# Kernel for a gated mix of a state-space convolution and a spectral filter: the order of work in its last part

## The chip, the cores and the metric

The kernel runs on one core of a Trainium2 chip. The metric is the device time of one execution in microseconds (us). The kernel before was timed three times: 625.73, 626.65 and 628.19 us; the median is 626.65. The execution that was profiled took 633.86 us, of which 631.9 us lie between its first and its last instruction (the span).

## What is computed

The input u has 2048 positions and 640 channels. Two branches work on it, and a gate per position mixes them. This is the reference, cut to what matters:

```
def _A_ref(u, log_A_real, A_imag, C_real, C_imag, log_dt, D_skip):
    dt = jnp.exp(log_dt)
    A = -jnp.exp(log_A_real) + 1j * A_imag
    C = (C_real + 1j * C_imag) * dt[:, None]
    P = jnp.exp((A * dt[:, None])[:, :, None] * pos[None, None, :])
    K = 2.0 * jnp.einsum("dn,dnl->dl", C, P).real
    Kf = jnp.fft.rfft(K, 2 * L)
    Uf = jnp.fft.rfft(u_t, 2 * L)
    y = jnp.fft.irfft(Uf * Kf[None], 2 * L)[:, :, :L]
    return y.transpose(0, 2, 1) + u * D_skip

def _B_ref(x, w_r, w_i):
    X = jnp.fft.rfft2(x, axes=(-2, -1)) * (w_r + 1j * w_i)
    return jnp.fft.irfft2(X, s=(S, D), axes=(-2, -1))

g = sigmoid((u * gate_w).sum(-1, keepdims=True))
return g * _A_ref(u, ...) + (1 - g) * _B_ref(u, w_r, w_i)
```

## The kernel before

All Fourier transforms are written as matmuls with tables of sines and cosines, in two stages each (32 blocks by 64 positions). The channels are worked in four parts of 160; the index c below names the part. Much is handed from stage to stage through DRAM.

The first two thirds of the span belong to parts that the change hardly touches: the forward transform of u, stored as the tensor u_d; the whole spectral branch up to its last inverse stage, stored as s3e_d; and the convolution kernel K, stored as k_d. `phase_c` then starts the transform of K for c = 0. `phase_d` is the last part of the program, from about 440 us on, and it is this part that the change rewrites.

`phase_d` has 16 units (c, u): four parts of the channels, and four groups of frequencies u within each. A unit goes through these steps.

- **Load**: `load` brings the spectra of u for this unit into the tile us (three buffers), on ScalarE's DMA queue (L813, L815).
- **First stage of K** (`T.first`, which runs `stage1`, L365 and L366): ten groups of matmuls for each c, spread over the four units of c - 1. ScalarE copies each group from PSUM into the tile t1. The tile kt that feeds it is loaded by `load_k` on SyncE's queue.
- **Front** (`fronts`): `spectra` makes a group of frequencies with four matmuls (L378; the one group 16 has two, L822). VectorE multiplies it by us twice (L835, L836), and for every two groups VectorE subtracts (L838) and GpSimd adds (L839); the product is the tile t2.
- **Back** (`backs`): the first inverse stage, 32 matmuls into a PSUM tile pi of four banks with one buffer (L855), two copies by ScalarE into s3 (L858, two buffers), and a store to the tensor s3_d on ScalarE's queue (L859).

Two kinds of last stages run beside the units. `last_e` takes the tile t3e, which `load_e` loads from s3e_d (L890), in six groups of two matmuls for each c (`halved`, L190), and VectorE writes each group times 1 - g to oe (L912). `last_c` takes the tile t3, which `load_c` loads from s3_d in four pieces (L902), in six groups for each c (L929); the result times g plus oe is the output (L934, L935, L932), which is stored.

PSUM has one pool, ps, of four banks for everything but the back; spectra, first stages and last stages take its banks in turn.

What sets the order: each unit's streams (fronts and backs; last stages; first stages) are generators, and `merge` draws from them by given times, which fixes only the order of the program's text. The tile framework then schedules: it orders each engine's instructions by its own estimates, so that an engine's order differs from the text. `behind(T.mm)` asks that a last stage be issued after the latest back's matmul. Backs follow their fronts by two units (`late`), from unit 13 on by one. Queues are in order: an instruction that waits holds all that stand behind it on its engine, and the same goes for DMA issues on SyncE's queue (SP) and on ScalarE's.

After the last unit comes the close: remaining backs, loads of the last pieces of t3, `last_c` for c = 2 and then for c = 3, and their stores.

Of the kernel before, what the change touches and what calls it, by code (L numbers as in the profile page):

```python
# [15 lines left out]
SYNC = mybir.DependencyInfo(mybir.DependencyClass.Sync, mybir.DependencyReason.DATA)  # L16
DRAM = bass.MemoryType.DRAM
# [165 lines left out]
class Ctx:  # L183
    pass

# [580 lines left out]
def phase_c(tc, A, T, ctx):  # L766

    nc = tc.nc
    V, G, S = nc.vector, nc.gpsimd, nc.scalar
# [6 lines left out]
    T.t1, T.kt, T.ki = {}, {}, {}  # L776
    T.w3 = T.cc.tile([128, 17, 2, 64], F32, name="w3")

    def load_k(c, h):
        if c < 4:  # L780
            T.kt[c, h] = T.kp.tile([128, 20, 64], F32, tag="k", name="kt")
            T.ki[c, h] = nc.sync.dma_start(T.kt[c, h][:, :, :], T.k_d[c, :, 20 * h:20 * h + 20])

    def first(c, ps):
        t1 = T.t1[c] = T.tp[c % 2].tile([128, 16, 160, 2], F32, tag="t1", name="t1")
        t1v = t1.rearrange("p x d y -> p d x y")
        for h in range(2):
            yield from stage1(nc, ps, T.e1, lambda q: T.kt[c, h][:, q, :], 20, t1v[:, 80 * h:80 * h + 80], S.copy)
            load_k(c + 1, h)

    T.load_k, T.first = load_k, first
    load_k(0, 0)
    load_k(0, 1)
    with tc.tile_pool(name="c_ps0", side="right", reuse_waits="tile", bufs=3, space=PSUM) as ps:
        yield from first(0, ps)


def phase_d(tc, A, T, ctx, out):
    nc = tc.nc
    V, G, S, P = nc.vector, nc.gpsimd, nc.scalar, nc.tensor  # L800
# [9 lines left out]

    def load(c, u, st):
        us = st.us = up.tile([128, 5, 2, 160], F32, tag="us", name="us")
        nc.scalar.dma_start(us[:, 0:4], T.u_d[c, :, 4 * u:4 * u + 4])  # L813
        if u == 2:
            nc.scalar.dma_start(us[32:64, 4], T.u_d[c, 32:64, 16])  # L815
# [9 lines left out]
    def fronts(c, u, st):  # L825
        t2 = st.t2 = wk.tile([128, 5, 2, 160], F32, tag="t2", name="t2")
        gs = GROUPS[u]
        for h in range(0, len(gs), 2):
            hn = min(2, len(gs) - h)
            l = slice(0, 128) if hn > 1 else slice(32, 64)  # L830
            ma = wk.tile([128, 2, 2, 160], F32, tag="ma", name="ma")
            mb = wk.tile([128, 2, 2, 160], F32, tag="mb", name="mb")
            for i in range(hn):
                pv = spectra(c, gs[h + i])[l]
                V.tensor_tensor(out=ma[l, i], in0=pv, in1=st.us[l, h + i], op=ALU.mult)  # L835
                V.tensor_tensor(out=mb[l, i], in0=pv, in1=st.us[l, h + i, ::-1, :], op=ALU.mult)  # L836
                yield 0.55
            V.tensor_tensor(out=t2[l, h:h + hn, 0], in0=ma[l, :hn, 0], in1=ma[l, :hn, 1], op=ALU.subtract)  # L838
            G.tensor_tensor(out=t2[l, h:h + hn, 1], in0=mb[l, :hn, 0], in1=mb[l, :hn, 1], op=ALU.add)  # L839

    def backs(c, u, st):
        t2, gs = st.t2, GROUPS[u]
        s3 = w2k.tile([128, 4, 320], F32, tag="s3", name="s3")
        p = pi.tile([128, 4, 512], F32, tag="pi", name="p_i2")
        for j in range(2):
# [7 lines left out]
            for ri in range(2):  # L853
                for o, l, i in todo:
                    T.mm = P.matmul(o, T.w3[l, gs[i], ri], t2[l, i, ri], start=ri == 0, stop=ri == 1)  # L855
            yield 0.55
        for s in (0, 2):
            S.copy(s3[:, s:s + 2], p[:, s:s + 2, 0:320])  # L858
        T.sd = nc.scalar.dma_start(T.s3_d[c, 32 * u:32 * u + 32].rearrange("(x k) a d -> (k a) x d", k=4), s3.rearrange("p s (j d) -> p (s j) d", j=2))  # L859
        yield 0.1  # L860

    groups = [(c, u) for c in range(4) for u in range(4)]
    late, sts, t3s, t3es, oes = [], {}, {}, {}, {}

    def mains(i):

        for y in groups[i + 1 if i else 0:i + 2]:
            sts[y] = Ctx()
            load(*y, sts[y])
        x = groups[i]  # L870
        yield from fronts(*x, sts[x])
        late.append(x)
# [140 lines left out]
```

## Time and profile before

| what | value |
|---|---|
| time, median of three | 626.65 us (625.73 to 628.19) |
| the profiled execution's own time | 633.86 us |
| its span | 631.9 us |
| mean granted TensorE clock | 0.926 |
| TensorE (PE) busy | 540.1 us (85%) |
| VectorE (DVE) busy | 463.1 us (73%) |
| ScalarE (ACT) busy | 362.9 us (57%) |
| GpSimd (POOL) busy | 235.8 us (37%) |
| HBM, read and written | 157 GB/s over the span |

The shares are means over the span. A page of the profile also shows the span in 40 slices of 15.8 us; the last twelve of these are `phase_d`, and in them the engines are busy by turns. What bounds that part is read from its stretches and from the chain of work that ended last: each step of this chain is followed back to what released it. In a row of the chain stand the start, the length and the piece of work, with its tile and line. In a table of stretches stand, for each engine, the busy us and in brackets the number of instructions, then the granted TensorE clock (1.00 is full speed), the mean busy share of the 16 DMA engines and GB/s. "PEld" is TensorE's loading of weights.

### The profile page before, as it was taken

The numbers are of one execution on the slowest core, as the hardware profiler recorded it, in microseconds if no ns is written. First come the engines' busy times: TensorE is split into PE (matmuls) and PEld (weight loads), VectorE is DVE, ScalarE is ACT, GpSimd is POOL, SyncE is SP. The second block draws the span as 40 slices with busy tenths as digits, with TensorE's granted clock in tenths as the row PEclk, the third lists the DMA queues.
The fourth block names the chain that finished last, engine by engine and source line by source line (L and its number), as shares of the span: only waits on it lengthen the run. The fifth ranks groups of instructions, "written<-read, shape, count | busy, mean of one in ns | idle before, by whom it ended". The sixth has DMA issues, their size and how long they took to land.

```text
span 631.9 us, 17674 instructions
## 1 busy us (share of the span) xinstructions
PE 540.1 (85%) x7580; PEld 396.9 (63%) x7580; DVE 463.1 (73%) x780; ACT 362.9 (57%) x655; POOL 235.8 (37%) x214
## 2 busy tenths in 40 slices
PE   9687979988989989987989988999499659849974
PEld 7675647765757666766776855668377446636641
DVE  6960597597899999999989899783376328408853
ACT  4644675486857689796878887977123211311220
POOL 4921153053436436344255253152122126107341
PEclk9888998999979999999879999979799959959987
DMA  8776203236612413232502320046848846764896
GB/s 341 304 272 211 65 27 123 90 128 194 229 43 63 135 44 113 84 135 65 154 2 72 92 107 23 26 137 214 319 146 311 286 139 219 289 204 146 271 303 244
DMA packets 47334, 100.66 MB, mean 159 GB/s; under 512 B 3204, under 2 KB 32280, under 8 KB 45368
## 3 DMA queue, kind: packets, MB, share of 16 engines
q1 hardware_dynamic: 24600, 66.69, 30.6%
q10 hardware_dynamic: 19616, 22.19, 10.9%
q0 software_dynamic: 3040, 10.65, 5.0%
q8 instruction: 60, 0.98, 0.6%
q14 instruction: 18, 0.15, 0.1%
HBM read 59.70 MB, written 39.81 MB: 157 GB/s over the span
## 4 chain that ended last, share of the span: by engine, by line
PE 53%; DVE 20%; DMA 14%; issue 5%; ACT 5%; POOL 2%; DVEq 0%; SPq 0%; ACTq 0%; POOLq 0%
PE p_s L365 9%; PE p_s L378 9%; PE p_eo L581 7%; PE p_e L668 5%; DMA t3e<-s3e_d 4%; PE p_k L725 4%; DMA s_d<-s 4%; DMA u_d<-ut 4%; DVE q L682 3%; PE p_e L190 3%; PE p_i L855 3%; PE p_t L532 3%; PE p_p L679 2%; PE p_c L929 2%; PE p_i L595 2%
## 5 line engine op out<-in xcount | busy, mean ns | idle before, releaser
L378 PE MATMUL p_s<-t,w 128*64 128x160 f32 x1040 | 97.3, 324 | 10.6 <-ACT ut L412 7.5
L378 PEld LDWEIGHTS p_s<-t,w 128*64 128x64 f32 x1040 | 77.1, 144 | 24.3 <-ACT ut L412 8.4
L710 POOL TENSOR_TENSOR y<-e,sc 128x512 f32<-128x512 f32 x40 | 55.5, 1386 | 93.9 <-DVE x L705 52.5
L670 ACT ACTIVATE e<-p_e 128x512 f32<-128x512 f32 x120 | 68.6, 601 | 23.6 <-PE p_e L668 21.4
L366 ACT COPY t<-p_s 128x512 f32<-128x512 f32 x40 | 24.4, 618 | 89.7 <-PE p_s L365 89.7
L725 PE MATMUL p_k<-x,y 128*32 128x64 f32 x2560 | 63.4, 227 | 11.1 <-POOL y L710 6.1
L581 PE MATMUL p_eo<-td,pmt 107*128 107x321 f32 x204 | 68.7, 457 | 3.0 <-ACT pmt L535 3.0
L712 POOL TENSOR_TENSOR y<-e,sc 128x512 f32<-128x512 f32 x40 | 55.4, 1386 | 41.2 <-ACT sc L696 31.2
L725 PEld LDWEIGHTS p_k<-x,y 128*32 128x32 f32 x2560 | 45.4, 112 | 40.0 <-issue 24.0
L839 POOL TENSOR_TENSOR t<-mb 128x320 f32<-128x320 f32 (+1 forms) x36 | 34.6, 962 | 79.0 <-DVE mb L836 65.1
L682 DVE SCALAR_TENSOR_TENSOR q<-q,p_p 128x512 f32<-128x512 f32 x80 | 53.1, 678 | 12.8 <-ACT q L681 12.5
L668 PE MATMUL p_e<-rm,par 128*128 128x512 f32 x120 | 59.6, 525 | 3.2 <-ACT e L670 3.0
L835 DVE TENSOR_TENSOR ma<-p_s,us 128x320 f32<-128x320 f32 (+1 forms) x68 | 33.1, 487 | 35.8 <-PE p_s L378 35.6
L681 ACT ACTIVATE q<-p_p 128x512 f32<-128x512 f32 x80 | 46.6, 592 | 6.0 <-PE p_p L679 5.6
L581 PEld LDWEIGHTS p_eo<-td,pmt 107*128 107x128 f32 x204 | 38.7, 199 | 17.9 <-ACT pmt L535 5.2
L707 DVE TENSOR_TENSOR x<-e,cx 128x1024 f32<-128x1024 f32 x40 | 48.4, 1210 | 1.6 <-ACT cx L698 1.6
L365 PEld LDWEIGHTS p_s<-c,kt 128*64 128x64 f32 x640 | 39.5, 144 | 14.0 <-issue 11.2
L679 PE MATMUL p_p<-rp,par 128*128 128x512 f32 x80 | 43.5, 549 | 5.0 <-DVE q L682 4.9
L929 PE MATMUL p_c<-t,c 128*64 128x480 f32 (+1 forms) x96 | 23.9, 615 | 25.9 <-issue 20.1
L858 ACT COPY s<-p_i 128x640 f32<-128x640 f32 x32 | 20.6, 695 | 44.1 <-DMA s_d<-s 18.5
L365 PE MATMUL p_s<-c,u 128*64 128x128 f32 x640 | 43.1, 285 | 2.5 <-ACT ut L412 2.5
L365 PE MATMUL p_s<-c,kt 128*64 128x128 f32 x640 | 43.9, 285 | 0.9 <-ACT q L681 0.7
(152 smaller groups left out, 1105.6 us busy)
## 6 DMA issues: line engine op xcount, KB each, us to landing
u_d<-ut SPq DMA_DIRECT2D x32, 320.0 KB, 3.2
us<-u_d ACTq DMA_DIRECT2D x16, 640.0 KB, 6.0
s_d<-s ACTq DMA_DIRECT2D x16, 640.0 KB, 5.7
t<-s_d SPq DMA_DIRECT2D x14, 640.0 KB, 6.3
ww<-in_w_l SPq DMA_DIRECT2D x8, 642.0 KB, 4.0
ue<-u_d SPq DMA_DIRECT2D x8, 640.0 KB, 4.3
k_d<-kt SPq DMA_DIRECT2D x4, 1280.0 KB, 8.7
kt<-k_d SPq DMA_DIRECT2D x8, 640.0 KB, 5.3
```

What stands on the lines that cost most here:

```text
L365: nc.tensor.matmul(p[64 * ri:64 * ri + 64, j, :], src(i + j), e1[ri], start=True, stop=True)
L378: ins = nc.tensor.matmul(p[64 * j:64 * j + 64, i, 160 * ri:160 * ri + 160], w2[:, x, 64 * ri:64 * ri + 64], t1[:, x // 2 if x < 32 else K0 ...
L581: P.matmul(p[:, :E], st.pmt[:DC, c, w, j, :], tv[:DC, w, c, :], start=c == 0, stop=c == 2)
L668: P.matmul(p[:, :], pars[t], rm[:, c:c + 512], start=True, stop=True)
L670: st.exp = S.activation(ef[:, c:c + 512], p[:, :], AF.Exp)
L679: P.matmul(p[:, :], pars[t], rp[:, c:c + 512], start=True, stop=True)
L681: S.activation(qf[:, c:c + 512], p[:, :], AF.Copy, bias=MAGIC)
L682: V.scalar_tensor_tensor(out=qf[:, c:c + 512], in0=qf[:, c:c + 512], scalar=MAGIC, in1=p[:, :], op0=ALU.subtract, op1=ALU.subtract)
L707: V.tensor_tensor(out=x[:, 0].rearrange("p d (h j) -> p d h j", h=2), in0=e[:, :, 0:64].rearrange("p d (h j) -> p d h j", h=2), in1=cx.uns ...
L710: ins = G.tensor_tensor(out=y[:, 1], in0=e[:, :, 64:96], in1=sc[:, 0], op=ALU.mult)
L712: G.tensor_tensor(out=y[:, 0], in0=e[:, :, 64:96], in1=sc[:, 1], op=ALU.mult)
L725: P.matmul(st.pb[32 * r:32 * r + 32, o, :], y[:, ri, 4 * qq + JR[r], :], x[:, ri, 4 * qq + JR[r], :], start=t % 2 + qq + 1 - ri == 0, stop ...
```

## The change

`phase_d` is written as one loop over the 16 units, and every engine keeps the order of that text. For this, the class `Pinned` wraps an engine: each instruction gets an order-only dependence (NOSYNC, which makes no wait on a semaphore) on the one issued before it through the same wrapper. Instructions made in `phase_d` therefore carry line L197, the line of the wrapper, in the changed kernel.

In the loop, the back of unit n - 1 (`inverse`) stands in the middle of unit n. Last stages move to later units: `last_e` stands in the third and fourth unit of c = 0, and in the second and third of each further c; `last_c(c - 1)` has its first half in the fourth unit of c and its second half in the first unit of c + 1. The loads of us are issued two units ahead (the first three by SyncE, in `phase_c`), and the table w3 is loaded in `phase_c` too, ahead of them. In the close, all loads of t3 are issued by SyncE.

```
+class Pinned:
+    def __init__(self, tc, eng):
+        self.tc, self.eng, self.last = tc, eng, None
+    def __getattr__(self, name):
+        f = getattr(self.eng, name)
+        def call(*args, **kw):
+            ins = f(*args, **kw)
+            if self.last is not None:
+                self.tc.add_manual_dep(ins.ins, self.last.ins.name, NOSYNC, reason="order")
+            self.last = ins
+            return ins
+        return call
...
 def phase_c(tc, A, T, ctx):
...
+    def load_u(eng, c, u):
+        if c < 4:
+            us = T.us[c, u] = T.up.tile([128, 5, 2, 160], F32, tag="us", name="us")
+            eng.dma_start(us[:, 0:4], T.u_d[c, :, 4 * u:4 * u + 4])
+            if u == 2:
+                eng.dma_start(us[32:64, 4], T.u_d[c, 32:64, 16])
...
     load_k(0, 1)
+    nc.sync.dma_start(T.w3[:, :, :, :], A["t_w3s"].rearrange("p (g r m) -> p g r m", g=17, r=2))
+    for u in range(3):
+        load_u(nc.sync, 0, u)
...
 def phase_d(tc, A, T, ctx, out):
...
+    nc = PinnedCore(tc)
...
+    def pair(c, u, h):
...
+        pvs = [spectra(c, g)[l] for g in gs]
+        for i in range(n):
+            V.tensor_tensor(out=ma[l, i], in0=pvs[i], in1=us[l, h + i], op=ALU.mult)
+            V.tensor_tensor(out=mb[l, i], in0=pvs[i], in1=us[l, h + i, ::-1, :], op=ALU.mult)
+        V.tensor_tensor(out=t2[l, h:h + n, 0], in0=ma[l, :n, 0], in1=ma[l, :n, 1], op=ALU.subtract)
+        G.tensor_tensor(out=t2[l, h:h + n, 1], in0=mb[l, :n, 0], in1=mb[l, :n, 1], op=ALU.add)
...
-        while len(late) > (1 if i > 12 else 2):
-            yield from backs(*late[0], sts.pop(late.pop(0)))
...
-            if g - (c == 0) in (0, 1):
-                beside = [last_e(c, AG * (g - (c == 0)))]
-            if c and g == 1:
-                load_c(c - 1, 0, 64)
-            if c and g == 2:
-                load_c(c - 1, 64, 64)
-            if c in (1, 2) and g > 1:
-                beside += [last_c(c - 1, AG * (g - 2))]
...
+    for n, (c, g) in enumerate(units):
+        if g == 0:
+            fst = T.first(nc, c + 1, ps) if c < 3 else iter(())
+        if g == 1 and c:
+            for u in range(3):
+                load_c(c - 1, u)
+        if g == 2 and c:
+            load_c(c - 1, 3)
+        if n == 15:
+            load_c(3, 0)
+        beside = []
+        if g - (c == 0) in (1, 2):
+            beside = last_e(c, AG * (g - 1 - (c == 0)))
+        elif g == 3 and c < 3:
+            beside = last_c(c - 1, 0)
+        elif g == 0 and c > 1:
+            beside = last_c(c - 2, AG)
+        beside = iter(beside)
+        pair(c, g, 0)
+        next(fst, 0)
+        if n and n < 14:
+            T.load_u(S, *units[n + 2])
+        next(beside, 0)
+        pair(c, g, 2)
+        next(fst, 0)
+        if n:
+            inverse(*units[n - 1])
+        next(beside, 0)
+        if len(GROUPS[g]) > 4:
+            pair(c, g, 4)
+        if g != 2:
+            next(fst, 0)
+        next(beside, 0)
+        for _ in beside:
+            pass
+        if g - (c == 0) == 2:
+            load_e(c + 1)
+    inverse(3, 3)
+    load_c(3, 1)
+    load_c(3, 2)
+    load_c(3, 3, 2)
...
```

Three places show what the change does to the engines' orders. The first is TensorE's order at the first last stage of the spectral branch (p_e from the tile t3e). Before, in the second unit:

```order
L365 MATMUL p_s_5650<-c_65,kt 64x128 x8
L378 MATMUL p_s_5666<-t_5276,w_68 64x160 x4
L855 MATMUL p_i_5827<-t_5592,w_5268 64x160 x32
L190 MATMUL p_e<-t3e,c_65 64x480 x2
L365 MATMUL p_s_5678<-c_65,kt 64x128 x8
```

Now, in the second unit and at the start of the third (p_s from t is a group of spectra, p_s from kt a group of the first stage, p_i the back):

```order
L197 MATMUL p_i_5723<-t_5595,w_5268 64x160 x32
L197 MATMUL p_s_5761<-c_65,kt 64x128 x8
L197 MATMUL p_s_5774<-t_5284,w_68 64x160 x4
L197 MATMUL p_s_5779<-t_5284,w_68 64x160 x4
L197 MATMUL p_s_5790<-c_65,kt 64x128 x8
L197 MATMUL p_e<-t3e,c_65 64x480 x2
```

The p_e group stood right behind the back of the first unit; now the rest of the second unit and half of the third lie between the two. From the first group of spectra to this p_e there were five groups of spectra, three of the first stage and a back; now there are ten, seven and a back.

The second place is TensorE's order at the first last stage of the convolution branch (p_c from the tile t3, here t_6083 or t_6110). Before, with c = 1, behind the first group of spectra of its third unit:

```order
L378 MATMUL p_s_6215<-t_5602,w_68 64x160 x4
L855 MATMUL p_i_6296<-t_5965,w_5268 64x160 x32
L855 MATMUL p_i_6405<-t_6089,w_5268 64x160 x32
L929 MATMUL p_c<-t_6083,c_65 64x480 x2
L365 MATMUL p_s_6228<-c_65,kt 64x128 x8
L378 MATMUL p_s_6238<-t_5602,w_68 64x160 x4
```

Now, in the fourth unit of c = 1:

```order
L197 MATMUL p_s_6359<-t_5614,w_68 64x160 x4
L197 MATMUL p_s_6364<-t_5614,w_68 64x160 x4
L197 MATMUL p_s_6375<-c_65,kt 64x128 x8
L197 MATMUL p_c<-t_6110,c_65 64x480 x2
L197 MATMUL p_s_6395<-t_5614,w_68 64x160 x4
L197 MATMUL p_s_6400<-t_5614,w_68 64x160 x4
```

Before, two backs in a row and then p_c stood ahead of the rest of the third unit, which stands behind p_c in the queue; now p_c stands one unit later, and no two backs stand together until the close.

The third place is SyncE's queue, which issues these loads. Before (k_d is the last store of K, t3 the piece that p_c needs):

```order
L735 DMA k_d_60<-kt_4654 128x2560
L890 DMA t3e_5585<-s3e_d_58 128x2560
L902 DMA t3_6083<-s3_d_59 32x5120
L782 DMA kt_5733<-k_d_60 128x1280
L890 DMA t3e_5863<-s3e_d_58 128x2560
L782 DMA kt_5942<-k_d_60 128x1280
L902 DMA t3_6083<-s3_d_59 32x5120 x2
```

Now:

```order
L761 DMA k_d_60<-kt_4654 128x2560
L197 DMA t3e_5593<-s3e_d_58 128x2560
L197 DMA kt_5759<-k_d_60 128x1280
L197 DMA kt_5994<-k_d_60 128x1280
L197 DMA t3e_6000<-s3e_d_58 128x2560
L197 DMA t3_6110<-s3_d_59 32x5120 x3
```

The first piece of t3 no longer stands ahead of the loads of kt and of the second t3e; three pieces of t3 follow each other behind them.

More of the change, by code (lines that the diff above doesn't have):

```diff
@@ L979, in phase_d @@
-    for y in late:
-        run(backs(*y, sts[y]))
-    with behind(T.sd):
-        load_c(3, 64, 32, eng=nc.scalar)
-    load_c(3, 96, 32, 2)
-    run(last_c(2, 0))
-    run(last_c(2, AG))
+    units = [(c, u) for c in range(4) for u in range(4)]
+    load_e(0)
+    for n, (c, g) in enumerate(units):
[35 more added lines that the diff above has]
+            load_e(c + 1)
```

154 lines of the change are left out of this document (55 added, 99 removed).

## The prediction

> **What bounds the kernel now.** I read the slices of the page first, then the chain of waits, then the stretches that the chain points to.
>
> ```profile
> span 631.9 us, 17674 instructions
> PEclk9888998999979999999879999979799959959987
> ```
>
> The granted clock drops to 5 in two of the last twelve slices. The chain says why; it starts for my purpose at the last part's first spectra (the timeline's row, 440.05).
>
> ```profile
> 440.05 0.79 PE L378 MATMUL p_s<-t,w 128*64 128x160 f32 x8 [0.51 <-ACT t L366]
> ```
>
> ```profile
> 441.06 13.91 DMA t3e<-s3e_d
> ...
> 494.79 11.49 DMA t3e<-s3e_d
> 506.28 6.60 issue
> 512.89 1.87 PE p_c L929 x4
> 514.76 1.71 PE p_s L365 x16
> 516.47 2.13 PE p_s L378 x16
> ...
> 549.87 9.42 DMA s_d<-s
> 559.29 4.81 issue
> ...
> 598.22 7.93 DMA s_d<-s
> ...
> 607.56 2.52 PE p_i L855 x64
> ```
>
> Between the waits the chain runs on TensorE alone. It stops four times: at the first t3e, twice ahead of a p_c whose t3 is not there, and at a store of s3. "issue" behind the transfers is the rest of the same waits: the piece of t3 can only be loaded once the store has landed. SyncE's own waits say it too:
>
> ```profile
> SPq L902 <- DMA s_d<-s: 105.0, 12, 15.3
> ```
>
> Next, the stretches (PE, PEld, DVE, ACT, POOL busy, clock, DMA share, GB/s):
>
> ```profile
> 441.00:632.00 191.00, 145.16 (x2214) 102.51 (x2210) 100.95 (x231) 39.17 (x62) 55.80 (x57) 0.86 0.71 241
> 441.00:455.00 14.00, 6.03 (x142) 5.50 (x138) 5.01 (x12) 3.18 (x5) 2.05 (x2) 0.83 0.99 388
> 495.00:513.00 18.00, 4.75 (x180) 3.49 (x176) 1.01 (x3) 4.46 (x7) 0.24 (x1) 0.77 0.92 309
> 550.00:564.00 14.00, 3.70 (x128) 2.90 (x128) 0.10 (x1) 2.57 (x4) 0.00 (x0) 0.59 0.88 282
> 523.00:543.00 20.00, 19.75 (x271) 14.29 (x269) 14.37 (x33) 5.01 (x8) 9.89 (x11) 1.00 0.81 277
> 465.00:495.00 30.00, 30.00 (x476) 22.50 (x474) 22.85 (x52) 8.15 (x14) 8.44 (x9) 1.00 0.70 237
> 611.40:632.00 20.60, 9.71 (x44) 3.44 (x40) 9.66 (x23) 0.00 (x0) 5.74 (x5) 0.81 0.74 264
> ```
>
> TensorE is idle for 8.0, 13.3 and 10.3 us in the three stalls, while DMA works hard; where TensorE flows, DMA has a rest (0.70, 0.81). So the last part is bound by turns: TensorE where it flows, transfers where it stops.
>
> **The change, part by part.** With the fixed order, p_e and p_c stand a unit and more behind the moves that feed them. I rebuild the last part from TensorE's rows at full clock:
>
> ```profile
> 520.86 0.69 PE p_s L822 x4
> ...
> 530.52 0.81 PE p_e L190 x4
> 531.32 0.87 PE p_s L365 x16
> 532.20 1.14 PE p_s L378 x16
> ...
> 545.42 0.73 PE p_i L855 x32
> 546.15 0.69 PE p_e L190 x4
> ...
> 548.53 0.02 issue
> ```
>
> A pair of spectra costs 1.14, a first-stage group 0.87, a last-stage group of 480 columns 0.81 and one of 320 columns 0.69, a back 2 x 0.73 = 1.46, group 16 0.69. From unit 0 to the last back the new order holds 32 pairs (36.5 us), 30 first-stage groups (26.1), 24 last-stage groups of 480 (19.4) and 12 of 320 (8.3), 16 backs (23.4) and four of group 16 (2.8): 116.5 us. `last_c` of c = 2 and 3 lies in the close, as before.
>
> How much longer than such a sum does a flowing stretch take? From 512.89 to 548.53 the old order ran 8 groups of 480 and 4 of 320, 9 first-stage groups, 15 spectra, the matmuls of two backs and one group 16: 6.5 + 2.8 + 7.8 + 8.6 + 2.9 + 0.7 = 29.3 us. It took 35.6, of which the first three rows, at the low clock, are 1.87 + 1.71 + 2.13 - (0.81 + 0.87 + 1.14) = 2.9 too long. That leaves 32.7, a factor of 1.12. Part of that excess is backs cut into single matmuls between other groups, which the new order keeps whole; I take 1.10, with 1.00 and 1.12 as ends. So 116.5 becomes 128 us (116.5 to 130.5), and unit 0's start at 440.05 plus 128 is 568.
>
> For the rest of the sum I need ScalarE's copies of the back and the landing times of loads:
>
> ```profile
> t3e<-s3e_d SPq DMA_DIRECT2D x4, 1280.0 KB, 7.2
> us<-u_d ACTq DMA_DIRECT2D x15, 640.0 KB, 6.2
> w<-in_t_w3s SPq DMA_DIRECT2D x1, 1088.0 KB, 10.0
> L858 ACT COPY s<-p_i 128x640 f32<-128x640 f32 x32 | 20.6, 695 | 44.1 <-DMA s_d<-s 18.5 <-PE p_i L855 16.7 <-DVE oe L912 7.2
> ```
>
> Behind the last unit comes the close. The last back waits for ScalarE's two copies of the one ahead, 2 x 0.70 by the row above, about 1.5 with its signals. From the end of the last back (607.56 + 2.52 = 610.08) to the end of the span there were 21.8 us: copies, store, load, two matmul groups, the last multiply-adds, the store of the output. The change leaves this chain alone, and the stall at 598.22 goes: the s3 buffer then waited for was held by a store two backs old, and now backs are a unit apart.
>
> What the new order moves into the way: **t3e for c = 1** is issued behind the last p_e of unit 3, and needed in unit 5. Between stand three pairs, four first-stage groups and a back, 3.4 + 3.5 + 1.5 = 8.4 us, or 9.2 with the factor. Such a load took 11.5 us in the chain above (7.2 in the middle, by the same rows). The cost is between 0 and 2.3 us; I take 1.5, nearer to the 11.5, since three pieces of t3 and a kt go with it. The first t3e lands at 455 as before or up to 6 us sooner, since w3 and two tiles us (2.4 MB, at 388 GB/s) now go ahead of 441; it is needed after 5.7 + 6.1 + 1.5 = 13.3 us of rows, 14.6 with the factor, at 454.7: nothing. The other loads have a unit or two: a unit is 8 us, a load 6.
>
> VectorE, ScalarE and GpSimd do the same work as before. In the flowing 30 us from 465 they were busy for 22.9, 8.2 and 8.4 us beside TensorE's 30.0, so they hide; if VectorE lost that cover, it could become the bound only where it has over a third more to do.
>
> The sum: 440.05 + 128 + 1.5 + 1.5 + 21.8 = 593 for the span, 39 less than 631.9, and 595 for the profiled execution's own time of 633.86. That execution was 7.2 us above the median of the runs, so I carry the 39 over: 626.65 - 39 = **588**. Its own range runs from a factor of 1.00 and no new wait (575) to 1.12 with the wait (591), and a little beyond for what no row shows.
>
> One rule speaks against this. The Trainium skill, "TensorE: Matmul & The Clock Gate", section "A second HAM failure mode: psum-queue depth-cycling", says that a kernel that cycles through PSUM banks can leave TensorE idle so often for moments that its clock swings between half and full. The new order cycles through four banks all along. This trace speaks against the rule here: from 465 to 495 the same four banks were cycled and the clock was 1.00. By the row the sum is as above; by the rule it would grow as in the last rival below.
>
> **The rivals.**
>
> *Transfers become the bound.* From 441 on DMA was busy 0.71 x 191 = 136 us. About 7 of them (2.4 MB at 277 / 0.81 = 342 GB/s) move ahead of 441, and 0.74 x 20.6 = 15 lie in the close, which leaves 113 to be done in 128 us, a share of 0.88. For it: the best 20 us in which TensorE flowed had 0.81. Against it: 0.99, 0.92 and 0.88 in the stalls, so a deep queue gives more. At 0.81 the middle takes 140 us: 440 + 140 + 23 = 603, or 598 by the median.
>
> *The waits only move.* If the t3 loads left SyncE so late that p_c waited again at its new place, only the first stall (8.0 us), its slow clock (2.9) and the close's 7.9 would be gained: 626.65 - 19 = 608. For it: SyncE is one queue, and three pieces stand behind t3e. Against it: the stores they wait for are two units old by then.
>
> *Slower: ScalarE's queue.* ScalarE issues the loads of the tile us and the stores of s3 between its copies, now in a fixed order, and a DMA issue that has to wait (for a buffer, or for an earlier transfer to be counted) holds the next first-stage copy, whose bank TensorE needs. If each unit waited for one landing there, 16 x 6.2 = 99 us would come on top: 588 + 99 = 687. It decides from 39 / 16 = 2.4 us a unit. For it: ScalarE waited three times for s3 stores, 18.5 us (its row above). Against it: those waits were for backs that followed at once; the buffers asked for now are two and three units old.
>
> *Slower: the clock.* Half clock over a third of the rows would take back the 39 us; over all of them the time would be 588 + 116.5 = 704. The rows at 1.00 speak against it.
>
> **How the numbers follow.** The forecast gets 0.65, transfers as the bound 0.18, moved waits 0.09, ScalarE's queue 0.06, the clock 0.02. The range runs from 574, just under the sum with no excess, to 606, which holds the transfer case with a slice of the moved waits: about 0.82. A measurement of this kernel can tell some 0.5%, 3 us, from no change. Faster: 0.65 + 0.18 + most of the moved waits = 0.90; slower: the two last, part of the time, 0.07; the same 0.03.
>
> **What would show it.** In the changed profile the last part's chain should be TensorE rows with no DMA piece over 3 us until the last back, which should end near 570; the clock should stay at 1.00 from about 445; DMA should hold 0.85 or more in each 25 us of the middle. p_c's waits ("issue" ahead of L929) should be gone from 500 to 565. If DMA stands at 0.9 or more with TensorE waiting for tiles us or t3, the transfers bound it; if ScalarE's idle time is put down to DMA for more than 2.4 us a unit, the gain is gone. I would be wrong at the root if the start at 440 moved, since the loads moved ahead of it share their queue with kt.

## The result, and the profile after

The changed kernel took 585.29 us (median of four runs, 578.36 to 589.73). The kernel before, run on the same chip beside it, took 627.42 us (625.73 to 632.62). The ratio is 0.924, with a 95% interval of 0.913 to 0.936: 7.6% faster. This ratio comes from the fast runs alone (those within 1.5% of their kernel's fastest), of the changed kernel 578.36 and 583.24 us (the two medians above divide to 0.933, six more runs below gave 0.927, and two executions of 1198.12 and 992.73 us further down stay out of their ratios in the same way). The profiled execution of the changed kernel took 587.33 us.

| what | before | after |
|---|---|---|
| span of the profiled execution | 631.9 us | 585.5 us |
| first spectra of the last part | 440.05 | 442.36 |
| end of the last back | 610.08 | 562.96 |
| between the two ("the middle" below) | 170.0 us | 120.6 us |
| from there to the end of the span ("the close") | 21.8 us | 22.5 us |
| mean granted TensorE clock | 0.926 | 0.961 |

The middle gave 49.4 us; the start lost 2.3 and the close 0.7, which makes the 46.4 us between the spans. The page of the changed kernel says the same in its slices (14.6 us each, so the last ten are the last part):

```profile
span 585.5 us, 17666 instructions
PEclk9989797999998998998989799999999999999997
DMA  9877211406461241233324023300287799999995
```

The clock shows no 5 any more, and DMA, which worked hard only in the stalls before, now stands at 9 in seven slices in a row. The chain of waits of the changed kernel (start, length, piece of work) runs through the middle like this:

```profile
442.36 9.13 PE p_s L197 x144
451.50 1.30 PE p_i L197 x64
...
455.82 0.81 PE p_e L197 x4
...
467.08 2.28 PE p_i L197 x64
...
479.23 0.81 PE p_e L197 x4
...
496.18 0.81 PE p_c L197 x4
...
557.83 2.34 PE p_i L197 x64
...
561.53 1.43 PE p_i L197 x64
...
564.30 4.23 DMA s_d<-s
```

The three places at which the chain before showed transfers of 13.91 and 11.49 us and an issue gap of 6.60 us (the first p_e, the second t3e, the first p_c) are rows of TensorE now, each begun the moment that TensorE got there. The first transfer in the chain is a store in the close. The stretches of the changed kernel (PE, PEld, DVE, ACT, POOL busy, clock, DMA share, GB/s):

```profile
441.00:585.50 144.50, 130.53 (x2246) 95.87 (x2240) 100.63 (x231) 40.88 (x65) 55.06 (x57) 0.97 0.90 311
442.40:455.00 12.60, 12.60 (x245) 12.15 (x247) 8.74 (x22) 5.23 (x9) 4.15 (x4) 1.00 0.97 356
455.00:475.00 20.00, 20.00 (x340) 15.23 (x344) 15.55 (x37) 6.01 (x11) 5.61 (x6) 1.00 0.73 226
475.00:495.00 20.00, 20.00 (x395) 15.70 (x389) 13.29 (x31) 8.15 (x13) 5.53 (x6) 1.00 1.03 386
563.00:585.50 22.50, 10.48 (x48) 3.71 (x46) 9.66 (x23) 1.27 (x2) 5.74 (x5) 0.82 0.68 231
```

The first row answers to the row 441 to 632 of before. TensorE's idle time in it fell from 191.00 - 145.16 = 45.8 us to 144.50 - 130.53 = 14.0, nearly all of it in the close (22.50 - 10.48 = 12.0). Its busy time fell from 145.16 to 130.53 for about as many matmuls, while the mean clock rose from 0.86 to 0.97: of some 46 us, 32 were standing still and nearly 15 were slower work. The first three rows behind each of the first three stalls of before were 2.8 to 2.9 us too long at the low clock, 8.6 us together; what else is in the 15 was not split up. In the middle TensorE is busy nearly all the time, and so, except from 455 to 475, are the transfers: two resources near their ends at once. (A share of 1.03 can't be a share of time; the DMA column is read here as a measure of load.) Which of them is the bound is the first question for the experiments.

SyncE still waits for stores of s3 (before: 105.0 us, 15.3 the longest), but in the middle the list of waits shows no engine waiting for what SyncE loads. From that list:

```profile
SPq L197 <- DMA s_d<-s: 48.3, 10, 10.0
```

### The profile page after: what moved, and what is told of

It reads as the page before. It is cut to its first block, busy times and chain, and to the rows that moved or that the text cites. A ratio compares the mean times of both kernels' runs of the same rounds, so it can differ in the third digit from the quotient of the medians.

```text
span 585.5 us, 17666 instructions
## 1 busy us (share of the span) xinstructions
PE 522.4 (89%) x7580; PEld 388.0 (66%) x7580; DVE 462.8 (79%) x780; ACT 363.0 (62%) x655; POOL 236.0 (40%) x214
## 4 chain that ended last, share of the span: by engine, by line
PE 58%; DVE 20%; DMA 7%; ACT 6%; issue 5%; POOL 3%; SPq 1%; DVEq 0%; ACTq 0%; POOLq 0%
PE p_s L197 11%; PE p_eo L607 6%; PE p_s L391 5%; PE p_e L694 5%; PE p_k L751 5%; PE p_i L197 4%; DVE q L708 3%; PE p_e L197 3%; PE p_s L404 3%; PE p_i L621 3%; PE p_p L705 3%; DMA u_d<-ut 2%; PE p_d L574 2%; PE p_c L197 2%; PE p_t L558 2%
## 5 line engine op out<-in xcount | busy, mean ns | idle before, releaser
L751 PE MATMUL p_k<-x,y 128*32 128x64 f32 x2560 | 63.0, 226 | 14.6 <-POOL y L736 6.1
L197 POOL TENSOR_TENSOR t<-mb 128x320 f32<-128x320 f32 (+1 forms) x36 | 34.2, 950 | 71.3 <-DVE mb L197 57.9
L404 PE MATMUL p_s<-t,w 128*64 128x160 f32 x528 | 46.7, 319 | 9.8 <-ACT ut L438 8.8
L197 ACT COPY t<-p_s 128x512 f32<-128x512 f32 x30 | 18.8, 625 | 50.2 <-PE p_s L197 48.3
L404 PEld LDWEIGHTS p_s<-t,w 128*64 128x64 f32 x528 | 38.7, 141 | 16.4 <-ACT ut L438 9.7
L197 PEld LDWEIGHTS p_s<-t,w 128*64 128x64 f32 (+1 forms) x528 | 37.3, 134 | 13.4 <-issue 5.1
L197 DVE TENSOR_TENSOR ma<-p_s,us 128x320 f32<-128x320 f32 (+1 forms) x68 | 32.8, 483 | 16.9 <-PE p_s L197 16.4
L197 PE MATMUL p_s<-t,w 128*64 128x160 f32 (+1 forms) x528 | 44.8, 304 | 0.5 <-ACT t L392 0.5
L391 PEld LDWEIGHTS p_s<-c,u 128*64 128x64 f32 x640 | 38.3, 144 | 8.6 <-issue 4.8
L438 DVE COPY ut<-p_s 128x320 f32<-128x320 f32 (+1 forms) x41 | 19.0, 486 | 29.5 <-ACT ut L438 16.2
```

What stands on the lines that cost most here:

```text
L197: ins = f(*args, **kw)
L391: nc.tensor.matmul(p[64 * ri:64 * ri + 64, j, :], src(i + j), e1[ri], start=True, stop=True)
L404: ins = nc.tensor.matmul(p[64 * j:64 * j + 64, i, 160 * ri:160 * ri + 160], w2[:, x, 64 * ri:64 * ri + 64], t1[:, x // 2 if x < 32 else K0 ...
L751: P.matmul(st.pb[32 * r:32 * r + 32, o, :], y[:, ri, 4 * qq + JR[r], :], x[:, ri, 4 * qq + JR[r], :], start=t % 2 + qq + 1 - ri == 0, stop ...
```

## The experiments

The other questions were which part of the change carries the gain (the distance between a store and its last stage, the loads of us two units ahead, the fixed order itself), and on which engine the fixed order matters. All ratios are to runs of the kernel before on the same chip. As the time at which the last part starts differs by up to 12 us between profiles (see the end), kernels are compared by the middle, which is 120.6 us in the changed kernel.

**The changed kernel again**, as the measure of the rest.

> The changed kernel once more, without an edit, on the same chip as the three runs beside it. Expected: 585 us (578 to 590); 120 to 122 us from the first spectra of the last part to the end of the last back, and 22 to 23 us from there to the end of the span. What may differ from the first profile is the start of the last part (434 to 442 in the profiles so far). If the middle differed by more than 3 us from 120.6, comparisons of the middle between kernels would say little.

583.59 us (median of six), ratio 0.927 (0.921 to 0.933). The middle was 121.2 us, the close 21.8 (span 579.8). From its chain (first and last TensorE row of the middle) and its stretch:

```profile
436.80 9.13 PE p_s L197 x144
...
556.61 1.43 PE p_i L197 x64
```

```profile
436.80:558.04 121.24, 119.55 (x2178) 91.77 (x2180) 90.92 (x208) 38.42 (x61) 49.26 (x52) 1.00 0.94 327
```

Two executions agree in the middle within 0.6 us, and two kernels below that leave the middle's work as it is have 120.6 and 120.9, so differences of 2 us there can be read.

**Is TensorE the bound?** Every p_e group is computed twice into the same bank, which only adds work.

```
-            halved(nc, p[:, 0:n], T.e3e, t3es[c][:, a + i:a + i + n])
+            for _ in range(2):
+                halved(nc, p[:, 0:n], T.e3e, t3es[c][:, a + i:a + i + n])
```

> The changed kernel with every matmul of last_e issued twice into the same place: 16 groups of 0.81 and 8 of 0.69 us more on TensorE, 18.5 us, and not a byte more to move. Theory (TensorE bounds the last part): 16 to 20 us more than the changed kernel, 0.95 to 0.965 of before, and the DMA share of the middle falls from 0.97 to about 0.85. Rival (transfers bound it, TensorE has time to spare): under 6 us more.

603.33 us, ratio 0.958 (0.953 to 0.962). The stretches of the middle, first of the changed kernel, then of this one:

```profile
442.36:562.96 120.60, 119.15 (x2178) 91.54 (x2180) 90.97 (x208) 38.49 (x61) 49.32 (x52) 1.00 0.95 330
```

```profile
435.44:576.40 140.96, 137.20 (x2274) 100.00 (x2276) 92.08 (x208) 38.42 (x61) 49.33 (x52) 1.00 0.84 283
```

The 96 added matmuls have 18.5 us by the rows of the prediction (16 groups of 0.81 and 8 of 0.69); TensorE's busy time grew by 18.0 and the middle by 20.4. Work added on TensorE comes out one for one, while the share of the transfers falls to 0.84. So TensorE bounds the middle.

**Less work on TensorE.** The last six p_e groups move from units 13 and 14 into the close.

```
-        if g - (c == 0) in (1, 2):
+        if g - (c == 0) in (1, 2) and c < 3:
             beside = last_e(c, AG * (g - 1 - (c == 0)))
...
     load_c(3, 3, 2)
+    for a in (0, AG):
+        for _ in last_e(3, a):
+            pass
     for a in (0, AG):
         for _ in last_c(2, a):
```

> The last p_e groups (the spectral branch of c = 3: 4 groups of 480 columns and 2 of 320, 4 x 0.81 + 2 x 0.69 = 4.6 us of TensorE) move from units 13 and 14 into the close, ahead of the last stages of c = 2. Theory that TensorE is the bound of the middle: the middle gets shorter by 4 to 5 us, and in the close the groups fill time in which TensorE waits for the last store and load, so the close grows by less than 2 us: 2 to 5 us faster than the changed kernel. Rival, transfers are the bound of the middle: it stays within 1.5 us of 120.6, and the time is the same or up to 2 us longer. Rival, VectorE is the bound of the close (0.8 us of multiplication a group more there): the close grows by 3 to 5 us and eats the gain.

581.71 us, ratio 0.925 (0.919 to 0.932): not to be told from the changed kernel. The middle was 118.4 us, 2.5 shorter where 4.6 us of TensorE's work had gone. The same edit together with the one on the loads (below) shows where the rest stayed. Its stretch of the middle, and its chain at the last backs:

```profile
442.14:560.41 118.27, 115.03 (x2154) 89.95 (x2156) 87.91 (x202) 38.51 (x61) 49.38 (x52) 1.00 0.94 328
```

```profile
547.70 9.85 DMA s_d<-s
...
558.96 1.46 PE p_i L197 x64
```

TensorE's busy time fell by 4.1 to 4.5 us, as it should; its idle time grew from 1.5 or 1.7 to 3.2. Of that 0.8 us is at the last back, which waits 2.2 us for ScalarE's copy into s3, whose buffer a store holds for 9.85 us (6.2 is the median of s3's stores in the changed kernel). Another 1.0 is a stop inside an earlier back that the profile puts down to nothing. In the kernel with this edit alone that stop is there too (0.95 us), while its last back waits 1.4 us for ScalarE, as in the changed kernel. So with 4% less to do TensorE is still most of the bound; a store at the end of the middle is seen in one execution only.

**More transfers.** First with loads of 640 KB on GpSimd's queue, into one buffer.

```
+            more = xk.tile([128, 4, 2, 160], F32, tag="more", name="more")
+            G.dma_start(more[:, :, :, :], T.u_d[c, :, 4 * g:4 * g + 4])
```

> The changed kernel with 13 more loads of 640 KB, one in each of units 1 to 13, on GpSimd's queue into a tile that nobody reads: 8.3 MB more, 25 us of transfers at 340 GB/s, and nothing more for TensorE. Theory (TensorE bounds, but transfers are nearly as long: 0.97 busy from 475 to 563): the slack is under 5 us, and 15 to 25 us are lost, as waits of TensorE's groups for tiles us and t3, 0.95 to 0.97 of before. Rival (TensorE alone bounds, transfers have slack): under 6 us more.

594.24 us, ratio 0.942 (0.935 to 0.949); the middle was 135.0 us. But this one doesn't measure what it should:

```profile
470.34 11.29 DMA more<-u_d
...
511.11 12.42 DMA more<-u_d
```

Each added load waits for the one ahead of it, as they share a buffer, and holds GpSimd's additions for t2 behind it. The chain runs through that queue. It shows loads that take 11 to 12 us to land, no more.

So once more, with 480 KB on SyncE's queue and two buffers:

```
+        if n and n < 14:
+            more = xk.tile([128, 3, 2, 160], F32, tag="more", name="more")
+            Q.dma_start(more[:, :, :, :], T.u_d[c, :, 4 * g:4 * g + 3])
```

> Thirteen loads that nothing needs are added in units 1 to 13, 480 KB each (6.4 MB together), issued by SyncE at the end of the unit into two buffers of their own. No engine but SyncE has a thing to do with them. At the 350 GB/s of the middle they take 18 us of the queues, and the middle of the changed kernel leaves 118 x (1 - 0.95) = 6 us free. Theory, transfers are almost the bound beside TensorE: 10 to 15 us longer than the changed kernel, with waits for us, t3 or t3e in the chain. Rival, the queues still have room (a busy share is not a limit): under 4 us longer, and a chain of TensorE rows as before.

597.40 us, ratio 0.950 (0.944 to 0.956): 14 us by the medians on this chip. The middle, its chain and its stretch:

```profile
467.07 14.10 DMA us<-u_d
...
543.76 14.54 DMA s_d<-s
```

```profile
436.42:562.13 125.71, 120.05 (x2112) 91.74 (x2112) 89.53 (x204) 36.92 (x59) 47.74 (x51) 0.99 0.98 352
```

The middle grew by 4.5 to 5 us; the close by more, from 21.8 or 22.5 to 29.8 (562.13 to the end of the span at 591.9), perhaps as its loads and stores stood behind what the middle had left over. 6.4 MB more, 18 us of the queues at 352 GB/s, cost 12 us of the span (591.9 against 579.8), so the changed kernel has little room left for transfers. Not all of that need be the transfers' share, though. SyncE's queue also waited for the added loads themselves, with loads of t3 behind them, and this was not separated:

```profile
SPq L197 <- DMA more<-u_d: 15.5, 4, 8.1
```

The Trainium skill, "Perfetto Trace Analysis", section "Roofline", says that on trn2 a core that is the only one active at its memory is bounded by its 16 DMA engines, about 435 GB/s together. An estimate from that figure: the 44.2 MB that this kernel moved in its middle take 102 us and lie within TensorE's 120. No stretch of this run that was read came to that rate (395 GB/s from 543.7 to 558.3), and at a mean of 352 GB/s and a share of 0.98 loads landed after 14 us and TensorE waited for them.

**The distance between store and last stage.** Last stages one unit earlier, and with them the loads of t3 and t3e; the fixed order is kept.

```
         if g == 1 and c:
-            for u in range(3):
+            for u in range(4):
                 load_c(c - 1, u)
-        if g == 2 and c:
-            load_c(c - 1, 3)
...
-        if g - (c == 0) in (1, 2):
-            beside = last_e(c, AG * (g - 1 - (c == 0)))
-        elif g == 3 and c < 3:
-            beside = last_c(c - 1, 0)
-        elif g == 0 and c > 1:
-            beside = last_c(c - 2, AG)
+        if g - (c == 0) in (0, 1):
+            beside = last_e(c, AG * (g - (c == 0)))
+        elif g > 1 and c in (1, 2):
+            beside = last_c(c - 1, AG * (g - 2))
...
-        if g - (c == 0) == 2:
+        if g - (c == 0) == 1:
             load_e(c + 1)
```

> The changed kernel with its last stages moved to where they stood before: p_e one unit earlier, p_c one unit earlier, with the loads of t3 and t3e asked for as early as that allows; order still fixed. Theory (distance between a store, its load and its last stage is the gain): p_c then needs t3 some 8 us behind the last back's copies, while store and load took 5.7 + 6.3 us before, so TensorE waits about 4 to 10 us twice ahead of p_c, and 0 to 5 us at the first p_e, and 8 to 25 us are lost: 0.94 to 0.965 of before. Rival (the fixed order alone gains): within 4 us of the changed kernel, 0.93.

598.28 us, ratio 0.949 (0.944 to 0.953); the middle was 134.4 us, 13.5 longer. Two of the old stalls are back, at the first t3e and ahead of a p_c, and behind the second TensorE works at a low clock (1.87 us for a p_c group that takes 0.81 in the changed kernel):

```profile
436.03 9.97 DMA t3e<-s3e_d
...
524.85 3.10 issue
527.94 1.87 PE p_c L197 x4
```

TensorE stands 4.1 and 3.8 us there by its list of waits. In the 5.6 us behind each the clock is 0.53 and 0.52, and a last-stage group with the 32 matmuls of p_s after it takes 5.5 and 5.6 us instead of 2.8: together 5.5 us more. So of the 13.5 us some 8 are waiting and the rest is the clock.

**The distance of the loads of us.** One unit ahead instead of two:

```
-    for u in range(3):
+    for u in range(2):
         load_u(nc.sync, 0, u)
...
-        if n and n < 14:
-            T.load_u(S, *units[n + 2])
+        if n and n < 15:
+            T.load_u(S, *units[n + 1])
```

> The loads of us are issued one unit ahead instead of two (14 of them in the last part, two ahead of it). In the changed kernel's profile such a load lands 8.8 us after its issue (median), and a unit takes 7.5 us, with some 7 us between the issue and the first use. Theory, the distance of two units is what keeps TensorE fed now that an engine's order is fixed: a wait of about 2 us in each unit, 13 x 2 = 26 us longer than the changed kernel (10 to 40), with DMA rows of us in the chain. Rival, the queues get shorter with fewer loads in flight and the landing falls to the 6.2 us of the kernel before: under 5 us longer.

601.71 us, ratio 0.954 (0.942 to 0.965); the middle was 140.7 us, 19.8 longer, within the expected 10 to 40. It didn't lose 2 us in each unit, though; the loss comes in lumps. From its chain:

```profile
473.44 5.81 issue
...
515.94 12.58 DMA us<-u_d
...
540.30 9.12 DMA us<-u_d
...
554.53 9.14 DMA us<-u_d
```

The first gap stands ahead of a p_e, but its t3e had landed at 471.7, before TensorE came to it. That instruction also waits for VectorE, and VectorE was waiting for us, a load that took 11.0 us to land; the p_e began at 479.26, right behind VectorE's first two products:

```profile
478.27 0.49 DVE L197 TENSOR_TENSOR ma<-p_s,us 128x320 f32<-128x320 f32 x1 [8.48 <-DMA us<-u_d]
```

The other gaps come from 515 on, where loads of us take 9 to 12 us to land.

**The order that is fixed.** Without any fixed order, the same text:

```
-            if self.last is not None:
-                self.tc.add_manual_dep(ins.ins, self.last.ins.name, NOSYNC, reason="order")
-            self.last = ins
```

> The changed kernel without the order-only dependences: the scheduler is free again, the text is the same. On TensorE it leaves the order as it was but for single matmuls of a back that it pulls ahead of a group of spectra. Theory (the gain is where the text puts the last stages and loads, not the pinning): 0.92 to 0.94 of the time of before, at most 5 us above the changed kernel, from backs cut in two. Rival (the fixed order is what gains): 0.96 of before or more.

588.94 us, ratio 0.936 (0.931 to 0.940); the middle was 127.6 us, 6.4 to 7 longer. From its chain:

```profile
463.53 10.48 DMA t3e<-s3e_d
...
527.12 2.34 PE p_i L197 x64
...
530.82 0.75 PE p_i L197 x18
531.58 0.96 PE p_c L197 x4
```

The first loss is the second t3e, 10.48 us from its issue to its landing, while TensorE had 8 us of other work. TensorE stood 2.3 us for it, and then worked at a low clock: the p_e and the 32 matmuls of p_s behind it took 4.7 us instead of 2.8, so that this one load cost 4.1 of the 6.4 to 7. The stretch behind the wait:

```profile
474.10:479.00 4.90, 4.86 (x52) 4.20 (x60) 2.83 (x6) 0.17 (x1) 0.81 (x1) 0.65 0.88 294
```

SyncE's queue had two pieces of t3 and a kt right ahead of it here, and t3e ahead of the pieces in the changed kernel. My theory after this run was that SyncE's order is what the fixing is worth. Two runs put it to the test: only SyncE fixed, and all but SyncE.

```
-            setattr(self, e, Pinned(tc, getattr(tc.nc, e)))
+            setattr(self, e, Pinned(tc, getattr(tc.nc, e)) if e == "sync" else getattr(tc.nc, e))
```

> Only SyncE keeps the order of the text; the other engines are free, as in the kernel without any fixed order. Its queue then issues the second t3e ahead of the pieces of t3, as in the changed kernel. Theory, what the fixed order is worth lies in SyncE's queue alone: the 10.5 us wait for the second t3e of the unpinned kernel is gone, the middle takes 121 to 123 us (unpinned 127.6, changed kernel 120.6 and 121.2), the time is 580 to 588. Rival, TensorE's or ScalarE's order matters too: the middle takes 125 us or more.

```
-            setattr(self, e, Pinned(tc, getattr(tc.nc, e)))
+            setattr(self, e, Pinned(tc, getattr(tc.nc, e)) if e != "sync" else getattr(tc.nc, e))
```

> The opposite: every engine but SyncE keeps the order of the text. SyncE's queue then issues two pieces of t3 and a kt ahead of the second t3e, as in the unpinned kernel. Theory, SyncE's order alone decides: the wait for the second t3e stands in the chain with 8 to 11 us at about 463, the middle takes 126 to 129 us, the time is 587 to 593. Rival, SyncE's order costs nothing as long as the other engines keep theirs: no wait over 2 us, 120 to 122 us.

The theory fell both times. With SyncE alone fixed the time was 591.29 us, ratio 0.940 (0.935 to 0.944), and the middle 127.3; with all fixed but SyncE it was 584.52 us, ratio 0.927 (0.923 to 0.932), and the middle 120.9, that of the changed kernel. SyncE's queue with the order of the unpinned kernel, and TensorE at the second t3e, in the kernel with SyncE free:

```profile
460.91 0.33 SPq L902 DMA_DIRECT2D t3e<-s3e_d  x1
```

```profile
469.28 1.03 PE p_e L197 x4
```

In all three orders t3e leaves as soon as the last p_e of c = 0 frees its buffer, 28.5 us into the last part here, 28.7 in the unpinned kernel. Here it was there when TensorE came for it, 8.4 us later. What differs is how long it took to land, and that I can't put down to one thing.

What the other engines' order is worth is seen between the first p_e of c = 2 and that of c = 3, in us from the first spectra, worked out from the chains:

| first p_e of | changed, again | SyncE free | SyncE fixed | unpinned |
|---|---|---|---|---|
| c = 1 | 37.6 | 36.9 | 37.8 | 39.3 |
| c = 2 | 71.6 | 71.2 | 73.5 | 75.4 |
| c = 3 | 102.2 | 101.8 | 107.8 | 108.1 |
| end of the last back | 121.2 | 120.9 | 127.3 | 127.6 |

Both kernels in which the orders of TensorE, VectorE, ScalarE and GpSimd are free lose 2 to 4 us on that stretch (2.1 unpinned, 3.7 with SyncE fixed). TensorE's order there (p_i_6906 is one back, p_i_7000 the next one), first in the unpinned kernel, then in the changed one:

```
MATMUL p_s_6859<-c_65,kt 64x128 x8
MATMUL p_i_6906<-t,w 64x160 x32
MATMUL p_i_7000<-t,w 64x160 x9
MATMUL p_c_6872<-t,c_65 64x480 x2

MATMUL p_s_6859<-c_65,kt 64x128 x8
MATMUL p_c_6872<-t,c_65 64x480 x2
MATMUL p_s_6879<-t,w 64x160 x4
MATMUL p_s_6884<-t,w 64x160 x4
MATMUL p_s_6895<-c_65,kt 64x128 x8
MATMUL p_i_6906<-t,w 64x160 x32
```

The scheduler hoisted a back above p_c, and nine matmuls of the next one with it. The back's PSUM tile has one buffer, so TensorE stands until ScalarE has copied the first (the chain above: p_i ends at 529.46, goes on at 530.82). ScalarE's order was freed as well, and a load of us that waits for its buffer stood ahead of the next copies. From the unpinned kernel's waits from 524 to 545, and its stretch behind the two backs:

```profile
ACT s L197 <- DMA us<-u_d: 5.9, 1, 5.9
```

```profile
536.50:543.00 6.50, 6.19 (x100) 4.14 (x98) 6.50 (x13) 1.29 (x2) 5.18 (x7) 1.00 0.98 351
```

VectorE, third in the row, is busy for all of these 6.5 us: the work held up by the two backs comes in a lump, and at its end TensorE waits 0.3 us for VectorE. That is little; the stop between the two backs has 1.4 us and the cut of a back in two about 0.5, which makes the 2.1. The kernel with SyncE fixed has the same order and the same rows (two backs at 531.89 and 535.59, then VectorE), and its 1.6 us more on this stretch are the clock. The same stop of 1.4 us was followed by half clock here, and by a clock of 1.00 in the unpinned kernel:

```profile
535.60:538.90 3.30, 3.30 (x26) 1.66 (x28) 0.14 (x1) 0.00 (x0) 0.00 (x0) 0.50 1.01 370
```

So the late t3e and the clock behind it make most of the one kernel's loss, and a lost clock is a part of the other's, and that both middles come to 127 us is in part chance. The rest lies at other places. One and a half p_c groups, which both kernels draw from the close in between the last two backs, cost only some 0.4 us of it: they take 1.75 us where the changed kernel waits 1.4 for ScalarE.

**The start.** In the changed kernel TensorE stops in the middle of a p_k group ahead of the last part, with nothing that the profile shows to hold it; the loads moved ahead of the last part fill the queues at that moment. Two of them were moved behind the last store of k_d:

```
-    for u in range(3):
-        load_u(nc.sync, 0, u)
+    load_u(nc.sync, 0, 0)
...
+    T.load_u(Q, 0, 1)
+    T.load_u(Q, 0, 2)
     load_e(0)
```

> Two of the three loads of us that the change put ahead of the last part (1.28 MB) are issued by SyncE only after the last store of k_d, one of them ahead of the first kt, one behind it. Theory, the gap of 1.8 to 2.9 us in which TensorE stands in the middle of a p_k group at about 430 ("issue": nothing that the profile shows holds it) comes with the loads that fill the queues there (0.5 us with one load of us less ahead): it falls to under 1 us and the last part starts 1 to 2.5 us sooner after the landing of the first ue (281.5 us from that row in the changed kernel's two profiles). In the last part the first t3e is issued behind one or both of them and may cost 0 to 3 us. Time: 581 to 587. Rival, the gap has to do with the length of the program (code that has to be fetched), not with loads: it stays at 2 to 3 us.

583.26 us, ratio 0.925 (0.923 to 0.928); middle 120.6. And both edits together:

> Both edits together: the last p_e groups in the close, and two of the loads of us behind the last store of k_d. If both gains hold and add (2.5 us in the middle by the one, up to 2 us ahead of it by the other, less 1 to 2 us in the close): 578 to 583, about 2 us below the changed kernel, which is hardly more than these comparisons can tell. If the first t3e is late by it, the same as the changed kernel or 1 to 2 us longer.

580.24 us, ratio 0.922 (0.918 to 0.926). The stop at this place in the changed kernel, with the loads spread, and with both edits:

```profile
436.36 2.89 issue
```

```profile
436.11 0.26 issue
```

```profile
435.29 2.35 issue
```

The gap shrank in the first of these kernels and is back in the second, which issues the same loads in the same places. So the loads don't explain it, and it stays open. In all the profiles of kernels with the new text it stands behind the same 45 of the 64 matmuls of a p_k group. The kernel with both edits has the lowest median of all, but its interval overlaps that of the changed kernel: a gain of about 0.5% that these runs can't confirm.

## Why the prediction was right, and where its sizes were off

The forecast was 588.0, measured 585.29. The mechanism was the one foretold: the four waits go, TensorE runs through the middle, the clock stays up. The terms of the sum, against the changed kernel's profile:

| term | predicted | measured |
|---|---|---|
| start of the last part | 440.05 | 442.36 |
| TensorE's rows times the factor | 128 | 119.2 |
| second t3e | 1.5 | 0 |
| last back's wait for ScalarE | 1.5 | 1.4 |
| close | 21.8 | 22.5 |
| span | 593 | 585.5 |

- **The factor was mis-sized.** 116.5 us of rows took 120.6 - 1.4 = 119.2, a factor of 1.02 where 1.10 was taken from the old order's flowing stretch (1.12 at most). This is 8.8 us, more than the net error of 7.5. The text said that a part of that excess was cut backs, and it was: in the old stretch the matmuls of the two backs took 4.8 us in seven pieces where the sum has 2.9, which is 1.9 of the excess of 3.4; the rest was not traced. The 2.7 us by which the new order exceeds the sum have another cause. The sum gives every back the price of one, but the back of each c's third unit (the one with group 16) is longer: 2.28 us, as in the row at 467.08 of the chain above, against 1.30 and 0.15 more on the group behind it for the others. Four of them make 3.3. A factor read from the stretch that one is about to change belongs at its lower end.
- **The second t3e** cost nothing: 8.3 us after its issue TensorE found it there. In the unpinned kernel it took 10.48 and held TensorE for 2.3, so either end could come. But the range of 0 to 2.3 had no term for the clock behind such a wait, 1.8 us more in that kernel.
- **The start** moved 2.3 us later, and the text had named that as a sign of being wrong at the root. It was not, at this size, and the starts of the kernels with the same text up to there spread by more (last section). What part of it the moved loads have is not settled.
- **The carry to the median** hid the error: the span fell by 46.4 where 39 was forecast, but the profile of before was 6.4 us above its median and that of after 2.0, so that the medians differ by 42.1. The forecast is 2.7 us off in the time and 7.5 in the span; that the first is so close is in part luck.

Of what should show it: the chain has no transfer until the last back, the last back ends at 563 (foretold: near 570), the clock is 1.00 from the start of the middle, and p_c's waits are gone. DMA is above 0.85 except from 455 to 475, where it is 0.73.

Of the rivals, *transfers become the bound* was the one to take seriously. It did not come true: doubling TensorE's last stages shows TensorE as the bound, and with 4% taken off it the middle still gave 2.5 of some 4.5 us. The margin is small, since 6.4 MB more made TensorE wait; how small was not measured. The text counted 0.81 in the best old stretch as evidence for a low ceiling; under a steady load the share reached 0.95 with TensorE hardly waiting. *The waits only move* was refuted by the chain, and the kernel with its stages one unit earlier shows what the distance is worth (13.5 us of the middle). *ScalarE's queue* did not happen in the changed kernel. The mechanism is real, however: in the unpinned kernel a load of us on that queue held ScalarE's copies for 5.9 us once. *The clock*: in the middle four banks are cycled for 120 us, and the clock is 1.00 in every stretch from 442 to 563. The rule of the Trainium skill cited there ("TensorE: Matmul & The Clock Gate", section "A second HAM failure mode: psum-queue depth-cycling") did not show itself in this kernel.

How the gain is made up, by taking single parts back: the loads of us two units ahead are worth 19.8 us of the middle, the distance of the last stages 13.5, the fixed order 6.4 to 7, each from one or two profiles and with the low clock behind the waits in it. These don't have to add up to 49.4, as a part that is taken back also meets fuller or emptier queues.

## What to carry to other kernels

When a part is bound by turns, TensorE where it flows and transfers where it stops, put each load and each last stage far enough behind its source that both run at once; here one unit of 7.5 us was too short for landings of 9 to 12 us, and two were enough. Fixing the order paid on the compute engines taken together and gained no time on the queue that was suspected first. The trace shows one place of it, two backs in a row round a PSUM tile with one buffer, where TensorE waits for ScalarE; no run fixes TensorE or ScalarE alone. And count the clock with each wait: behind waits of 2 to 6 us TensorE's next groups took up to twice their time. Test such a suspicion by freeing one engine and by fixing one: only both together showed it.

## What the runs showed of the hardware

The time at which the last part starts differs by 12 us (432.4 to 444.8) between profiles of kernels with the same work up to there, and 8 us of that arise in the first 160 us (the first transfer of ue begins between 153.0 and 160.7). This transfer, in the chains of the changed kernel, of the same kernel again, and of the kernel before:

```profile
160.67 4.42 DMA ue<-u_d
```

```profile
155.34 4.57 DMA ue<-u_d
```

```profile
160.73 4.34 DMA ue<-u_d
```

The granted clock of that time differs too; which of the two makes the other is not shown. The first 100 us of the changed kernel, and of the same kernel again:

```profile
0.00:100.00 100.00, 81.73 (x1237) 65.02 (x1239) 62.19 (x90) 56.53 (x104) 42.48 (x39) 0.91 0.54 196
```

```profile
0.00:100.00 100.00, 82.73 (x1311) 66.23 (x1311) 67.25 (x99) 60.78 (x110) 44.09 (x41) 0.97 0.56 203
```

Counted from that row, the last part starts 279.3 us later in the kernel before, 281.7 and 281.5 in the changed one, and 279.0 to 286.3 in the other kernels with the new text whose chains show that row, so that a cost of the moved loads, if there is one, lies within this spread. What stops TensorE for 0.3 to 2.9 us inside a p_k group at about 430 to 440 in all the kernels with the new text, and not in the one before, was not found.
